# Scores in 64x64 and transposes with logits in 128x64 parts of the array, and loads requested three steps ahead

## The chip, the core and the metric

The kernel runs on one core of a Trainium2 chip. The metric is the device time of one execution in microseconds, the median of several runs. The profile is one execution taken by the hardware profiler; its times count from the start of that execution's span.

## What is computed

Three stages follow one another: decaying linear attention over 2 x 8 heads of 768 tokens, a mixture of 8 experts with one expert for each token and a capacity, and a feed-forward layer with a rational activation. The part that the change touches is the attention and the gate's logits:

```python
for t in range(S):                       # S = 768, D = 64, H = 8, B = 2
    state = gamma * state + einsum('bhd,bhe->bhde', k[:, :, t], v[:, :, t])
    y[:, :, t] = scale * einsum('bhd,bhde->bhe', q[:, :, t], state)
x = y.transpose(0, 2, 1, 3).reshape(B * S, H * D)
logits = x @ w_gate                      # then argmax, softmax, slot by count
h = relu(einsum('ecd,edf->ecf', disp, w1)); y = einsum('ecf,efd->ecd', h, w2)
h = x @ w_in; g = P(h) / Q(h); out = g @ w_out
```

## The kernel before

**Units and steps.** The attention is cut into 12 units of 128 tokens with all 8 heads (`NU` = 12, six for each batch). The loop in `attention` (L630) has one step for each unit `u`. Instructions are issued in the order in which the program writes them (`manual_schedule`), so each engine's order is the order of the calls below, and a call that waits holds back what stands behind it on its engine.

**The groups on TensorE.** For a unit there are five groups, each of matmuls in fp32 that the trace shows as two instructions each:

- `scores(u)` (L285): for four feature blocks j and two row halves r, 64 rows of k against 64 rows of q, giving 128 keys by 128 queries. Its result lies in a pair of banks ("s", for unit 1 "y"); `mask` on VectorE copies it out, and the next scores need the pair free.
- `inter(u)` (L313): the state from earlier units against q, in 64x64 parts of the array. `intra(u)` (L331): v against the masked scores, in 128x64 parts. Both add into the pair of banks "y", which `attn_xt` on VectorE reads into `xt`.
- `state(u)` (L299): k against v with 64 columns, in 128x64 parts; ACT copies it to SBUF for the next unit's inter. The last unit of a batch (u = 5) has none, and the first (u = 6) has no inter.
- `gate_mm(u)` (L351): `xt` against an identity with the gate's weights beside it (136 columns), which gives the transposed rows and the logits, in 128x128. ACT copies the logits to `lgs` and the rows to `xs` (`gate_out`), and SP stores `xs` to `xd` in HBM.

In step u the order on TensorE is scores(u+1), inter(u), intra(u), state(u), gate_mm(u-1); in steps 1 and 2 scores(u+1) come behind state(u).

**Loads.** SP's queue holds the kv loads (`attn_load`: q and k by feature in one half, v and k by token in the other, 512 KB each), the `xd` stores and the expert weights in parts of 512 KB (`load_next`, parts counted from 0, `LOADS[u]` of them in step u). A kv load of unit u+4 is written at the head of step u, into one of five buffers; it needs the buffer of unit u-1. POOL scales v of unit u+2 in step u (`scale`, L267), so a scaling that waits starts when the second half of that unit lands.

**Weights.** Each part is split in two: `split_hi` on ACT (`HI_AT`) and `split_lo` on VectorE (`LO_AT` at the head of a step, `LO_END` at its end). The six buffers of parts come free with `split_lo`.

**Routing.** The units form two groups, 0 to 6 and 7 to 11. When the logits of the first are there (step 7), VectorE works out the gate (`gate_parts`), ranks (`rank_pos`, step 8) and tables (`rank_put`, `gate_put`, step 9); `place_first` in step 10 multiplies them on TensorE (L502), copies the result out, makes the index (L533) and starts the early gather of 128 rows from `xd` on POOL (L871). Behind the loop `attn_tail` transposes these rows (`early_x`, L699), does the last gate_mm and begins with the first expert (`win_l1`, L756).

Of the kernel before, what the change touches and what calls it, by code (L numbers as in the profile page):

```python
# [7 lines left out]
F32 = mybir.dt.float32  # L8
# [16 lines left out]
NU = NT // 128  # L25
# [7 lines left out]
DEC0 = 10  # L33
LAG = (2, 3, 4, 5)
WA, WC = 7, 3
LOADS = (0, 1, 0, 1, 0, 1, 0, 2, 1, 1, 1, 2)
HI_AT = {4: (0,), 5: (1,), 8: (2,), 9: (3, 4), 10: (5,)}
LO_AT = {6: (0,), 7: (1,)}
LO_END = {9: (2,), 10: (3,), 11: (4,)}
NA = 48  # L40
LOAD_AT = {1: (34, 0), 2: (34, 1), 6: (35, 0), 7: (35, 1)}
DEC_STEPS = (14, 15, 16, 17, 18, 19, 21, 22, 25, 26, 27, 28, 29, 30, 31, 33)
# [38 lines left out]
class Build:  # L81
# [154 lines left out]
    def attn_load(self, u, c):  # L236
        nc = self.nc
        if c == 0:
            self.kv[u] = self.ap.tile([128, 4, 512], F32, tag="kv", name="kv", bufs=5)
        dst = self.kv[u][:, 2 * c : 2 * c + 2].rearrange("p w n -> p (w n)")  # L240
        nc.sync.dma_start(out=dst, in_=self.a["kv"][u, c])

# [41 lines left out]

    def scores(self, u):  # L285
        kt, qt = self.feats(u)
        sc = self.sc[u] = self.pair_bank("y" if u == 1 else "s", "sc").rearrange("p (r j t) -> p r j t", r=2, j=4)
        for j in range(4):
            for r in range(2):
                rows = slice(64 * r, 64 * r + 64)  # L290
                self.mm(sc[:, r, j], kt[rows, j], qt[rows, j], True, True)

    def mask(self, u):
        m = self.col("mask").unsqueeze(1).to_broadcast([128, 8, 128])
# [56 lines left out]
    def gate_mm(self, u):  # L351
        nc = self.nc
        xt = self.xt.pop(u)
        if u < NU - 1:
            banks = [self.bank(t, "xk") for t in ("lg", "xk")]
        else:
            y = self.pair_bank("y", "xk")
            banks = [y[:, 0:512], y[:, 512:]]
        self.xk[u] = [b[:, 0 : 2 * 136].rearrange("p (k n) -> p k n", k=2) for b in banks]
        for k in range(4):  # L360
            nc.tensor.matmul(self.xk[u][k // 2][:, k % 2], lhsT=xt[:, k], rhs=self.wi[:, k], start=True, stop=True)
        for half in range(2):
            out = self.lgs[:, u, 2 * half : 2 * half + 2]
            nc.scalar.activation(out=out, in_=self.xk[u][half][:, :, 128:], func=AF.Copy)
# [217 lines left out]
    def attention(self):  # L582
        nc, tc, a = self.nc, self.tc, self.a
        with ExitStack() as st:
            self.ap = self.pool("attn", stack=st)
            self.pa = self.pool("pa", space=PSUM, stack=st)
            self.kv, self.sc, self.scm, self.s, self.yt, self.xt = {}, {}, {}, {}, {}, {}
            self.route, self.place, self.xk, self.rk, self.where = {}, {}, {}, {}, {}
            self.qd, self.yp = {}, {}
            n0, n1 = self.cols["ident"][0], self.cols["tri"][0]  # L590
            self.ca = self.ap.tile([128, -(-n0 // 32) * 32], F32, name="ca")[:, 0:n0]
            self.wi = self.ap.tile([128, 4, 256], F32, name="wi")[:, :, 0:136]
            self.tri = self.ap.tile([128, 128], BF16, name="tri")
            self.ones = self.ap.tile([128, 128], BF16, name="ones")
            self.lgs = self.ap.tile([128, NU, 4, E], F32, name="lgs")
            self.xg0 = self.ap.tile([128, DM], F32, name="xg0")
            self.x0 = [self.ap.tile([128, 4, 128], F32R, name=n) for n in ("xh0", "xl0")]
            self.wu = self.ap.tile([128, 128], BF16, name="wu")
            nk = self.cols["gk"][0]
            self.attn_load(0, 0)  # L600
            nc.sync.dma_start(out=self.ca[:, 0:nk], in_=a["ct"][:, 0:nk])
            self.attn_part(0, 2)
            self.attn_part(0, 3)
            self.attn_load(1, 0)
            self.attn_part(1, 2)
            self.attn_part(1, 3)
            nc.sync.dma_start(out=self.ca[:, nk:n1], in_=a["ct"][:, nk:n1])
            self.attn_load(2, 0)
            nc.sync.dma_start(out=self.ct, in_=a["ct"][:, n0:])
            self.attn_load(2, 1)  # L610
            for c in range(2):
                self.attn_load(3, c)
            nc.sync.dma_start(out=self.ca[:, n1:], in_=a["ct"][:, n1:n0])
            dve, pool = nc.vector, nc.gpsimd
            dve.memset(self.wu, 0.0)
            dve.memset(self.ones, 1.0)
            self.warm(WA)
            self.scores(0)
            self.mask(0)
            for h in (0, 4):  # L620
                self.scale(0, dve, slice(h, h + 4))
            self.y_table(0, pool)
            self.scale(1, pool)
            self.y_table(1, pool)
            self.y_table(2, pool)
            self.warm(WC)
            ident = self.col("ident").unsqueeze(1).to_broadcast([128, 4, 128])
            wg = self.col("wg").rearrange("p (k e) -> p k e", e=E)
            done = {GROUPS[b + 1] - 1: b for b in range(len(GROUPS) - 1)}
            for u in range(NU):  # L630
                last = u == NU - 1
                if u + 4 < NU:
                    for c in range(2):
                        self.attn_load(u + 4, c)
                self.load_next(LOADS[u])
                if u + 2 < NU:
                    self.scale(u + 2, pool)
                if u + 3 < UPB:
                    self.y_table(u + 3, pool)
                for n in LO_AT.get(u, ()):  # L640
                    self.split_lo(n // 2, n % 2)
                if u == 0 or 2 < u < NU - 1:
                    self.scores(u + 1)
                    self.mask(u + 1)
                if u - 2 in done:
                    next(gate)
                self.inter(u)
                if u - 4 in done:
                    self.place_first()
                self.intra(u)  # L650
                if u:
                    self.attn_xt(u)
                if u - 2 in done:
                    next(gate)
                self.state(u)
                if 0 < u < 3:
                    self.scores(u + 1)
                    self.mask(u + 1)
                if u == 0:
                    self.attn_xt(0)  # L660
                    nc.scalar.activation(out=self.wi[:, :, 0:128], in_=ident, func=AF.Copy)
                    nc.scalar.activation(out=self.wi[:, :, 128:], in_=wg, func=AF.Copy)
                if u == 1:
                    nc.scalar.activation(out=self.tri, in_=self.col("tri"), func=AF.Copy)
                    nc.scalar.activation(out=self.b0a, in_=self.ab[:, 4:5], func=AF.Abs)
                    nc.scalar.activation(out=self.b1a, in_=self.ab[:, 5:6], func=AF.Abs)
                    nc.vector.memset(self.cq, 1.0 + 1e-6)
                if u:
                    self.gate_mm(u - 1)
                if u - 2 in done and not last:  # L670
                    self.rank_mm(done[u - 2])
                if u:
                    self.gate_out(u - 1, (0,))
                if u - 1 in done:
                    gate = self.gate_parts(done[u - 1])
                    next(gate)
                if u:
                    self.gate_out(u - 1, (1,))
                for n in HI_AT.get(u, ()):
                    self.split_hi(n // 2, n % 2)  # L680
                if u - 2 in done and not last:
                    self.rank_pos(done[u - 2])
                if u - 3 in done and not last:
                    self.rank_put(done[u - 3])
                    self.gate_put(done[u - 3])
                for n in LO_END.get(u, ()):
                    self.split_lo(n // 2, n % 2)
            self.attn_tail()
# [17 lines left out]

    def attn_tail(self):
        u, b = NU - 1, len(GROUPS) - 2
        self.early_x()
        self.gate_mm(u)  # L710
        self.early_lo()
# [2 lines left out]
        self.gate_group(b)  # L714
        self.gate_out(u)
        ps.append(self.pair_bank("y", "l1")[:, 0:512])
        self.load_next(1)
        self.rank_mm(b)
        self.rank_pos(b)
        self.h0 = self.wp.tile([128, 2, 512], F32, tag="wt", name="h0", bufs=3)  # L720
# [8 lines left out]
        n = E * (self.nsub + 1)  # L729
# [632 lines left out]
```

## Time and profile before

| what | us |
|---|---|
| median of 3 runs | 513.41 (513.2 to 513.69) |
| the profiled execution's time | 513.91 |
| its span | 512.1 |
| TensorE busy in the span | 500.3 (98%) |
| VectorE | 405.4 (79%) |
| ACT | 361.9 (71%) |
| POOL | 243.9 (48%) |

The span is what the profile covers; 1.8 us of the execution's time lie around it. Busy shares are means over stages of different kinds: the attention takes the first 60 us, the experts follow to about 230 us, then the feed-forward layer.

### The profile page before, as it was taken

The page shows a single profiled execution, that of the slowest core. Times are in us where ns is not written, and L with a number is a line of the kernel's source. Part 1 is how long each engine was busy: PE and PEld are TensorE (multiplying, and loading weights), DVE is VectorE, ACT ScalarE, POOL GpSimd, SP SyncE. Part 2 cuts the span into 40 slices and gives each one's busy share as a digit, 9 for nine tenths or more (in the row PEclk, how much of TensorE's full clock was granted, in tenths as well). Part 3 has the DMA queues.
Part 4 walks back from the last instruction along what each step waited for, and adds up shares of the span by engine and source line. Part 5 has one row for each costly group of instructions (what it writes and reads, how often), then busy time and mean ns, then how long its engine had stood idle before and what let it go on. Part 6 is the DMA issues. An engine that isn't in the chain of part 4 may idle for free.

```text
span 512.1 us, 9408 instructions
## 1 busy us (share of the span) xinstructions
PE 500.3 (98%) x3531; PEld 439.3 (86%) x3531; DVE 405.4 (79%) x588; ACT 361.9 (71%) x588; POOL 243.9 (48%) x187
## 2 busy tenths in 40 slices
PE   7999899999999999999999999999999999999995
PEld 4888777999999999999888888888888888888873
DVE  3468876788887978876696989999899998865973
ACT  1344537858686776855797989989899987776760
POOL 2531041033333547235354537767568765354774
PEclk9999999999999999999999999999999999999998
DMA  8999647988987999993400002222013100000203
GB/s 317 408 411 353 205 147 247 353 265 317 327 276 273 334 257 345 265 283 104 166 0 1 0 2 83 83 82 83 21 63 110 56 1 0 1 0 0 84 21 144
DMA packets 27554, 83.08 MB, mean 162 GB/s; under 512 B 4976, under 2 KB 5360, under 8 KB 27504
## 3 DMA queue, kind: packets, MB, share of 16 engines
q1 hardware_dynamic: 24448, 73.52, 42.4%
q0 software_dynamic: 2624, 7.35, 4.1%
q10 hardware_dynamic: 432, 1.57, 0.9%
q8 instruction: 28, 0.46, 0.4%
q14 instruction: 22, 0.18, 0.1%
HBM read 71.93 MB, written 10.49 MB: 161 GB/s over the span
## 4 chain that ended last, share of the span: by engine, by line
PE 65%; DVE 1%; POOL 1%; issue 1%; ACT 1%; POOLq 0%; DVEq 0%
PE h L1068 9%; PE h L1069 9%; PE h L1070 8%; PE o L1140 7%; PE o L1139 7%; PE o L1141 7%; PE l L950 3%; PE l L952 3%; PE l L979 3%; PE l L978 3%; PE l L951 3%; PE l L977 3%; POOL out L1170 1%; PE tp L921 1%; DVE fw L1105 0%
## 5 line engine op out<-in xcount | busy, mean ns | idle before, releaser
L148 DVE TENSOR_TENSOR wlo<-raw,whi 128x1024 fp32r<-128x1024 f32 x80 | 109.8, 1387 | 14.0 <-ACT whi L143 13.7
L1119 POOL TENSOR_TENSOR gg<-fx,gg 128x512 fp32r<-128x512 f32 x47 | 61.1, 1299 | 70.2 <-issue 62.4
L143 ACT ACTIVATE whi<-raw 128x1024 fp32r<-128x1024 f32 x80 | 83.2, 1054 | 3.5 <-PE l L978 3.4
L1068 PE MATMUL h<-yh,whi 128*128 128x512 f32 x192 | 74.9, 390 | 0.0
L1139 PE MATMUL o<-whi,gg 128*128 128x512 f32 x192 | 74.8, 390 | 0.0
L1070 PE MATMUL h<-yh,wlo 128*128 128x512 f32 x192 | 74.8, 389 | 0.0
L1069 PE MATMUL h<-yl,whi 128*128 128x512 f32 x192 | 74.7, 389 | 0.0
L1140 PE MATMUL o<-wlo,gg 128*128 128x512 f32 x192 | 74.7, 389 | 0.0
L1141 PE MATMUL o<-whi,gg 128*128 128x512 f32 x192 | 74.7, 389 | 0.0
L1094 POOL TENSOR_TENSOR fw<-fh,fw 128x512 f32<-128x512 f32 x48 | 64.3, 1339 | 13.5 <-ACT fw L1083 12.8
L203 POOL TENSOR_TENSOR gq<-gq 128x512 int32<-128x512 int32 x16 | 26.7, 1668 | 87.7 <-DVE gq L200 61.9
L1081 ACT ACTIVATE fx<-h,ct 128x512 f32<-128x512 f32 x48 | 37.3, 777 | 38.2 <-PE h L1070 38.1
L950 PE MATMUL l<-xh,whi 128*128 128x224 f32 x224 | 62.0, 277 | 0.1
L977 PE MATMUL l<-hh,whi 128*128 128x224 f32 x224 | 61.9, 276 | 0.0
L952 PE MATMUL l<-xh,wlo 128*128 128x224 f32 x224 | 61.5, 275 | 0.0
L979 PE MATMUL l<-hh,wlo 128*128 128x224 f32 x224 | 61.5, 274 | 0.0
L978 PE MATMUL l<-hl,whi 128*128 128x224 f32 x224 | 61.4, 274 | 0.0
L951 PE MATMUL l<-xl,whi 128*128 128x224 f32 x224 | 61.4, 274 | 0.0
L950 PEld LDWEIGHTS l<-xh,whi 128*128 128x128 f32 x224 | 43.0, 192 | 0.4 <-ACT yh L814 0.3
L978 PEld LDWEIGHTS l<-hl,whi 128*128 128x128 f32 x224 | 43.0, 192 | 0.1
L977 PEld LDWEIGHTS l<-hh,whi 128*128 128x128 f32 x224 | 43.0, 192 | 0.1
L951 PEld LDWEIGHTS l<-xl,whi 128*128 128x128 f32 x224 | 43.0, 192 | 0.0
(165 smaller groups left out, 1172.6 us busy)
## 6 DMA issues: line engine op xcount, KB each, us to landing
raw<-wm SPq DMA_DIRECT2D x61, 512.0 KB, 7.0
r<-wf SPq DMA_DIRECT2D x32, 512.0 KB, 4.9
kv<-kv SPq DMA_DIRECT2D x22, 512.0 KB, 6.9
wd<-gq SPq DMA_DIRECT2D x16, 256.0 KB, 6.2
raw<-wd SPq DMA_DIRECT2D x8, 512.0 KB, 6.5
xd<-xs SPq DMA_DIRECT2D x12, 256.0 KB, 5.4
raw<-wm ACTq DMA_DIRECT2D x3, 512.0 KB, 6.3
kv<-kv SPq DMA_DIRECT2D x4, 256.0 KB, 5.3
```

Source lines behind the costliest of these rows:

```text
L143: nc.scalar.activation(out=self.whi[i][:, sl], in_=raw, func=AF.Copy)
L148: (eng or self.nc.vector).tensor_tensor(out=self.wlo[i][:, sl], in0=raw, in1=self.whi[i][:, sl].bitcast(F32), op=ALU.subtract)
L950: nc.tensor.matmul(ps[:, fi], lhsT=wh[:, sl], rhs=xh[:, k], start=(k == 0), stop=False)
L951: nc.tensor.matmul(ps[:, fi], lhsT=wh[:, sl], rhs=xl[:, k], start=False, stop=False)
L977: mm(lhsT=wh[:, ws], rhs=fh, start=(f == 0 and o % 2 == 0), stop=False)
L978: mm(lhsT=wh[:, ws], rhs=fo, start=False, stop=False)
L1068: nc.tensor.matmul(h, lhsT=wh[:, sl], rhs=self.yh[:, k, ts], start=(k == 0), stop=False)
L1069: nc.tensor.matmul(h, lhsT=wh[:, sl], rhs=self.yl[:, k, ts], start=False, stop=False)
L1070: nc.tensor.matmul(h, lhsT=wl[:, sl], rhs=self.yh[:, k, ts], start=False, stop=(k == 3))
L1139: self.nc.tensor.matmul(ps, lhsT=gh[:, ms], rhs=wh[:, ws], start=first, stop=False)
L1140: self.nc.tensor.matmul(ps, lhsT=gh[:, ms], rhs=wl[:, ws], start=False, stop=False)
L1141: self.nc.tensor.matmul(ps, lhsT=gl[:, ms], rhs=wh[:, ws], start=False, stop=last)
```

## The change

- Scores are cut into two halves of 64 keys each, so 16 matmuls on 64x64 parts in place of 8 on 64x128; unit 1's scores go to the pair "s" as well.
- `gate_mm` is cut into two halves of 64 tokens, so 8 matmuls on 128x64 parts in place of 4 on 128x128.
- In step 0 scores(1) come behind intra(0), in step 3 scores(4) behind inter(3).
- kv loads are written three steps ahead from step 1 on, into four buffers instead of five.
- `place_first` moves from between inter and intra of step 10 to between state(10) and gate_mm(9).
- Weight loads: one moves from step 5 to 4, one from step 11 to 10, and the one of the tail to its head. `split_hi` of part 2 moves from step 8 to 6, `split_lo` of part 2 from the end of step 9 into step 7, ahead of the gate's reductions.

```diff
-LOADS = (0, 1, 0, 1, 0, 1, 0, 2, 1, 1, 1, 2)
-HI_AT = {4: (0,), 5: (1,), 8: (2,), 9: (3, 4), 10: (5,)}
+LOADS = (0, 1, 0, 1, 1, 0, 0, 2, 1, 1, 2, 1)
+HI_AT = {4: (0,), 5: (1,), 6: (2,), 9: (3, 4), 10: (5,)}
 LO_AT = {6: (0,), 7: (1,)}
-LO_END = {9: (2,), 10: (3,), 11: (4,)}
+LO_MID = {7: (2,)}
+LO_END = {10: (3,), 11: (4,)}
@@ attn_load
-            self.kv[u] = self.ap.tile([128, 4, 512], F32, tag="kv", name="kv", bufs=5)
+            self.kv[u] = self.ap.tile([128, 4, 512], F32, tag="kv", name="kv", bufs=4)
@@ scores
-        sc = self.sc[u] = self.pair_bank("y" if u == 1 else "s", "sc").rearrange("p (r j t) -> p r j t", r=2, j=4)
+        sc = self.sc[u] = self.pair_bank("s", "sc").rearrange("p (r j t) -> p r j t", r=2, j=4)
         for j in range(4):
-            for r in range(2):
-                rows = slice(64 * r, 64 * r + 64)
-                self.mm(sc[:, r, j], kt[rows, j], qt[rows, j], True, True)
+            for c in range(2):
+                keys = slice(64 * c, 64 * c + 64)
+                for r in range(2):
+                    rows = slice(64 * r, 64 * r + 64)
+                    self.mm(sc[keys, r, j], kt[rows, j, keys], qt[rows, j], True, True)
@@ gate_mm
-            nc.tensor.matmul(self.xk[u][k // 2][:, k % 2], lhsT=xt[:, k], rhs=self.wi[:, k], start=True, stop=True)
+            for c in range(2):
+                toks = slice(64 * c, 64 * c + 64)
+                self.mm(self.xk[u][k // 2][toks, k % 2], xt[:, k, toks], self.wi[:, k], True, True)
@@ attention
-                if u + 4 < NU:
+                if 0 < u < NU - 3:
                     for c in range(2):
-                        self.attn_load(u + 4, c)
+                        self.attn_load(u + 3, c)
...
-                if u == 0 or 2 < u < NU - 1:
+                if 3 < u < NU - 1:
                     self.scores(u + 1)
                     self.mask(u + 1)
...
                 self.inter(u)
-                if u - 4 in done:
-                    self.place_first()
+                if u == 3:
+                    self.scores(u + 1)
+                    self.mask(u + 1)
                 self.intra(u)
+                if u == 0:
+                    self.scores(u + 1)
+                    self.mask(u + 1)
...
+                if u - 4 in done:
+                    self.place_first()
                 if u:
                     self.gate_mm(u - 1)
...
                     self.gate_out(u - 1, (0,))
+                for n in LO_MID.get(u, ()):
+                    self.split_lo(n // 2, n % 2)
@@ attn_tail
+        self.load_next(1)
         self.early_x()
         self.gate_mm(u)
...
         ps.append(self.pair_bank("y", "l1")[:, 0:512])
-        self.load_next(1)
         self.rank_mm(b)
```

## Rows read from the trace of the kernel before

**Rows 1.** Waits of TensorE over the span: engine, line, releaser: total us, times, longest

```profile
PE sc L340 <- DMA kv<-kv: 2.2, 1, 2.2
PE tp L502 <- DVE rr L496: 1.2, 1, 1.2
PE yt L340 <- DVE xt L348: 0.7, 2, 0.5
```

**Rows 2.** Windows: stretch, us, busy of each engine, granted clock, DMA share, GB/s

```profile
40.00:45.00 5.00, 5.00 (x82) 4.49 (x82) 3.82 (x10) 1.88 (x8) 1.04 (x1) 1.00 1.02 407
...
54.00:56.00 2.00, 2.00 (x32) 1.74 (x28) 1.90 (x9) 0.57 (x2) 0.82 (x1) 1.00 0.06 23
```

**Rows 3.** Timeline of TensorE, step 7: start, us, out<-in, array part, columns, count

```profile
36.42 1.16 PE L340 MATMUL sc<-kv 64*128 64x128 f32 x16
37.51 0.67 PE L340 MATMUL yt<-kv,s 64*64 64x128 f32 x16
38.10 1.09 PE L340 MATMUL yt<-scm,kv 128*64 128x128 f32 x16
39.03 0.64 PE L340 MATMUL st<-kv 128*64 128x64 f32 x16
39.59 1.19 PE L361 MATMUL xk<-wi,xt 128*128 128x136 f32 x8
40.72 0.38 PE L340 MATMUL sc<-kv 64*128 64x128 f32 x2
```

**Rows 4.** Timeline of TensorE in narrow windows, 37.78 to 38.10

```profile
37.78 0.40 PE L340 MATMUL yt<-kv,s 64*64 64x128 f32 x8
...
37.89 0.29 PE L340 MATMUL yt<-kv,s 64*64 64x128 f32 x4
38.10 0.33 PE L340 MATMUL yt<-scm,kv 128*64 128x128 f32 x2
```

**Rows 5.** Timeline of the weight loads, step 7

```profile
38.10 0.85 PEld L340 LDWEIGHTS yt<-scm,kv 128*64 128x64 f32 x16 [0.17 <-POOL kv L267]
```

**Rows 6.** Timeline of step 0, VectorE and TensorE; brackets: idle before, releaser

```profile
6.48 0.75 DVE L267 TENSOR_TENSOR kv<-kv,ca 128x256 f32<-128x256 f32 x2
...
8.26 1.16 PE L340 MATMUL sc<-kv 64*128 64x128 f32 x16 [2.22 <-DMA kv<-kv]
```

**Rows 7.** Timeline of POOL: scaling of units 8 and 10

```profile
33.75 1.04 POOL L267 TENSOR_TENSOR kv<-kv,ca 128x512 f32<-128x512 f32 x1 [3.48 <-DMA kv<-kv]
...
42.11 1.04 POOL L267 TENSOR_TENSOR kv<-kv,ca 128x512 f32<-128x512 f32 x1 [4.17 <-DMA kv<-kv]
```

**Rows 8.** Timeline of VectorE, steps 7 to 10

```profile
41.04 0.55 DVE L393 TENSOR_REDUCE lg<-lgs 128x56 f32<-128x224 f32 x1 [1.10 <-ACT lgs L364]
...
42.24 0.98 DVE L398 TENSOR_TENSOR eq<-eq,ct 128x56 f32<-128x56 f32 x1
...
51.95 0.38 DVE L496 TENSOR_TENSOR rr<-at,gl 128x224 fp32r<-128x224 f32 x1
52.25 1.22 DVE L148 TENSOR_TENSOR wlo<-raw,whi 128x1024 fp32r<-128x1024 f32 x1
53.39 1.22 DVE L297 TENSOR_TENSOR scm<-sc,ca 128x1024 f32<-128x1024 f32 x1
...
54.73 0.15 DVE L533 TENSOR_SCALAR gidx<-tab 128x1 int32<-128x1 f32 x1
...
55.38 0.68 DVE L348 TENSOR_TENSOR xt<-yt,qd 128x512 f32<-128x512 f32 x1
```

**Rows 9.** Early gather: POOL, its landing; all gathers' landing; TensorE's transposes of it

```profile
55.17 1.20 POOL L871 DMA_INDIRECT xg<-xd,gidx  x1 [8.89 <-DVE tab L512]
...
xg<-xd,gidx POOLq DMA_INDIRECT x1, 3.6
...
DMA to landing us min/median/max: 3.4/6.5/7.6
...
58.86 0.64 PE L699 MATMUL xtp<-ct,xg 128*128 128x128 f32 x4
```

## The prediction

> **What bounds the kernel now.** I read the waits of TensorE over the whole execution first [rows 1]. They hold nearly all the time in which TensorE is not busy, about 5 us in 512.1, and all of it lies before 57 us, in the attention steps. What comes behind that point is a block that TensorE fills: its length I leave as it is, and the question is only how much earlier it starts. Its first instruction is the transposes of the early gather, at 58.86 [rows 9]. The stretches of the windows come next [rows 2]: in the attention steps the DMA engines are full (1.02 at 407 GB/s), and by 54 us they are empty (0.06). The granted clock is 1.00 in both, the 2.4 GHz level. Then step 7 of the unit loop group by group [rows 3], single groups inside it [rows 4], and last the VectorE and gather rows at the end of the attention [rows 8, 9].
>
> So three things are close to one another here: TensorE in every step, the DMA queue up to about 50 us, and VectorE from 41 to 56 us, where one instruction follows the other without idle time.
>
> **Shape changes on TensorE.** Step 7 takes 40.72 - 36.42 = 4.30 us [rows 3]. Four 64x64 pieces with 128 columns start together every 0.11 us (37.78 to 37.89 [rows 4]). At 0.11 per 128 columns the streaming alone is: scores 8 pairs x 0.11 = 0.88; inter 4 x 0.11 = 0.44; intra 8 x 0.11 = 0.88; state, 64 columns, 8 x 0.055 = 0.44; logits with transposes, 136 columns, 8 x 0.117 = 0.94; together 3.58. The other 0.72 us go to four changes of the array's shape. One can be seen: from the last inter group (37.89) to the first intra (38.10) pass 0.21 us, not 0.11 [rows 4]. Inter, entered and left by a change, takes 0.59 where it streams 0.44, so a change to 64-column weights costs 0.15; the two to 128-column weights then share 0.72 - 0.30 = 0.42, 0.21 each.
>
> After the change scores are 64x64 like inter, and the logits 128x64 like intra and state. Streaming stays: 32 score pieces in fours are 8 x 0.11, 16 logit pieces in pairs 8 x 0.117. Two changes are left (into scores, into intra), 0.30. A step falls from 4.30 to 3.88, **-0.42**. No row shows a 64x64 score. Its bounds: as inter's fours (rows 4, the same order of row halves inside column halves, the same split over banks and partitions), or, if only two ran at once, 16 x 0.11 = 1.76, +0.46 on the step. I take the fours.
>
> **The start.** Scores of unit 1 wait 2.2 us for k and q to 8.26 [rows 1, 6]; intra of unit 0 stands behind them though its v is scaled by 6.48 + 0.75 = 7.23 [rows 6]. Put ahead, its 0.93 [rows 3] fall into that wait: **-0.9**, nothing if v or the mask were late (they are not), so 0 to -0.9. Unit 1's scores move to the other pair of banks, whose reader is done by then: nothing.
>
> **Steps 1 to 6 on TensorE.** Steps 1 and 2 keep four changes, two of them narrower: -0.1 each. Step 3 saves 0.4 and the wait for the mask behind scores, 0.2. Step 4 saves 0.42, step 5 (no state) 0.4, step 6 (no inter) 0.25. With the start that is 0.9 + 0.2 + 0.6 + 1.07 = 2.8: scores of unit 8 could start at 36.42 - 2.8 = 33.6.
>
> **The loads.** Every kv load is now requested in the step after the one that requested it before, behind one more store of xd, and behind the weight load that moved up from step 5 to 4. Neither costs anything while the queue stays full, since a landing then goes by the bytes ahead; the cover is the full queue [rows 2], and if it runs dry each gap moves all that follows. At 407 GB/s 512 KB take 1.29 us, a 256 KB store 0.64. The second half of unit 8 lands at 33.75 (its scaling on POOL starts there [rows 7]), so the half with k and q at 32.46; one more weight load and one more store ahead give 34.4. So the DMA queue, not TensorE, sets step 7: **34.4, -2.0**. Unit 11: the second half of unit 10 (42.11 [rows 7]) plus one store is 42.75; two weight loads, a store and the half itself make it 42.75 + 3 x 1.29 + 0.64 = 47.3. TensorE's scores of unit 11 wait for that, which the wait for VectorE behind them (below) hides.
>
> **VectorE from step 7.** The low split of weight part 2 (parts counted from 0; 1.22, the form at 52.25 [rows 8]) moves from the end of step 9 into the 1.10 us in which VectorE waits for the logits at 41.04 [rows 8]; one change less shortens that gap by 0.2, so 0.3 stick out. The high split on ACT moves from step 8 to 6, where ACT waits for TensorE: nothing. The reductions then start at 41.04 - 2.0 - 0.1 = 38.9, **-2.1**. From there to 55.38 none of VectorE's 40 instructions has idle time ahead of it (first and last, [rows 8]); the tables are done at 51.95 + 0.38 = 52.33. So the faster TensorE of steps 8 to 10 gains nothing by itself: it waits for VectorE at the placement products, as now (1.2 [rows 1]). They stand behind state now; scores, inter, intra and state of step 10 run in the wait.
>
> **The early gather.** Before, tables, the split (1.14 to the next start), mask and copies led to the index at 54.73 + 0.15 = 54.88 [rows 8]. Now the split is gone from this chain (-1.14) but unit 10's xt stands ahead of the copies (+0.68): 54.88 - 2.1 - 1.14 + 0.68 = 52.3. The gather follows 0.29 later (55.17 [rows 9]), 52.6; it took 3.6 [rows 9] on empty DMA engines: 56.2. Here the cover is gone: weight part 8 is now requested in step 10, a step earlier, since its buffer's split no longer stands at the end of step 9. By bytes: from 42.75 eight loads (10.3) and four stores (2.6) end at 55.7, and the gather's own 0.64 gives 56.3. Both ways 56.3; the transposes start at 56.4 instead of 58.86: **-2.4**. TensorE would be there earlier: from the tables (52.33 - 2.1 = 50.2) through products (1.0), logits, inter, intra and logits (1.1 + 0.6 + 0.9 + 1.1) at 54.9. So it waits for the gather, a new wait.
>
> **The tail.** Transposes and expert weights stay 128x128, the last logits become 128x64: two changes more, 0.15 + 0.21: **+0.36**. The last weight request ahead of the final logits costs only the queue of SP, where the last xd store stands behind it; that store has until the next gathers, behind the first expert's first products. Sum -2.4 + 0.36 = **-2.0**. Within it some tenths are loose: POOL's scaling at 42.11 holds VectorE's multiply at 42.24 for 0.98 [rows 7, 8], and such meetings will fall elsewhere. Against the profiled execution: span 512.1 to 510.1, its time 513.91 to 511.9; the median of the runs is 0.5 below that one: **511.4**.
>
> **Rivals.**
> 1. *The gather meets the weight loads* (slower side). On loaded engines gathers took 6.5 in the median, 7.6 at most [rows 9]. Issued at 52.6 and landing 6.5 later, it is there at 59.1, against 58.8 now; with the tail's 0.36 that is 514.1; at 7.6, 515.2. It decides from a latency of 5.8: above, the kernel is slower. For it: weight part 8 goes out before the gather now. Against it: eight loads end by 55.7, and a gather queues only behind what is ahead of it. 18 in 100 (11 within 0.2%, 7 slower).
> 2. *The queue runs dry.* Requests a step later leave 3 us of gaps; unit 11's k and q come at 50.3, state of step 10 ends at 53.1, the index is known at about 54.6, the transposes start at 58.6, and with the tail nothing is left: 513.5. Rows 2 speak against it. 8 in 100.
> 3. *More is gained.* POOL's scaling no longer holds VectorE, and the gather is not held by loads: another 1.5, 509.9. If neither VectorE nor DMA bound anything, TensorE alone would give 2.8 + 0.4 x 3 + 1.2 = 5.2, 508.2. 10 in 100.
> 4. *The halves don't run beside each other.* If the weight loads of two column halves with the same rows were not hidden behind matmuls, the 0.85 that 16 such loads take [rows 5] would come on top of the logits in 12 steps: +10 on TensorE against its 5.2, 518. Against it: intra's 16 loads (0.85 [rows 5]) lie inside its 0.93 [rows 3]. 4 in 100, fours that run as pairs included.
>
> The Trainium skill, "TensorE: Matmul & The Clock Gate", Part 3, "The mechanism", has weight loads overlap running matmuls only where their row groups differ, which speaks against column halves of the same rows. By that rule rival 4 would be the forecast; rows 3 and 5 of this case disagree with it for intra.
>
> **How the numbers follow.** The forecast has 60 in 100, of which 8 fall within 0.2%. About 0.2%, 1 us, is what a measurement of this kernel can tell from no change. Faster: 52 + 10 = 62; within: 8 + 11 + 8 = 27; slower: 7 + 4 = 11. The range takes the gather at 6.5 us at its upper end (514.1) and rival 3 at its lower (509.9); beyond lie some 4 of rival 1 and the 4 of rival 4 above, and half of rival 3 below.
>
> **What would show it.** In the timeline of step 7 or later: scores in fours 0.11 apart, scores to inter without a gap, a step of streaming and two changes of 3.9. Scores of unit 8 waiting for a load near 34.4; the reductions near 38.9; placement products waiting for the tables; the gather issued near 52.6; TensorE waiting for it, transposes near 56.4. Wrong if that wait reaches 58.5, if scores run in pairs, if DMA shows gaps before 50 us, or if TensorE gets new waits after the transposes.

## The result and the profile after

The changed kernel takes **517.12 us** in the median of 4 runs (515.43 to 517.59), the kernel before 513.55 beside it (513.2 to 514.6): a ratio of **1.0062**, 95% interval 1.0046 to 1.0077 (the quotient of the two medians is 1.0070). It is slower, where 511.4, a gain, was forecast. The profiled execution of after is the fastest of its four: 515.43, span 513.6, against 513.91 and 512.1. So the trace explains 1.5 us of the 3.6 by which the medians differ.

What lies behind the attention steps is as long as it was: span less start of the early transposes is 513.6 - 60.20 = 453.4 after and 512.1 - 58.86 = 453.2 before [rows 9]. All is decided before 60 us, and the question is only why the transposes start 1.3 us later instead of 2.4 earlier.

Waits of TensorE over the span of after: engine, line, releaser, then total us, times, longest ("issue" is a stop for which the profile shows no releaser). They answer [rows 1].

```profile
PE sc L343 <- issue: 1.8, 3, 0.8
PE st L343 <- issue: 1.4, 1, 1.4
PE sc L343 <- DMA kv<-kv: 1.2, 2, 0.7
PE xtp L712 <- DMA xg<-xd,gidx: 1.1, 1, 1.1
...
PE rk L438 <- issue: 0.8, 1, 0.8
```

The waits of before are gone (scores of unit 1 for 2.2, placement products for 1.2). In their place stand three things that no row of before had: five stops with the releaser issue, 4.0 us together, a wait of scores for kv late in the attention (0.7, unit 11; the other of the two, 0.5, is what is left of unit 1's), and one of the transposes for the gather (1.1), which was forecast.

Timeline of TensorE in after: step 8 up to the start of step 9, which answers [rows 3]. Columns: start, us, then the instruction group.

```profile
41.07 1.10 PE L343 MATMUL sc<-kv 64*64 64x128 f32 x32
41.99 0.62 PE L343 MATMUL yt<-kv,s 64*64 64x128 f32 x16
42.54 1.09 PE L343 MATMUL yt<-scm,kv 128*64 128x128 f32 x16
43.46 0.63 PE L343 MATMUL st<-kv 128*64 128x64 f32 x16
43.93 1.10 PE L343 MATMUL xk<-wi,xt 128*64 128x136 f32 x16
44.96 0.20 PE L438 MATMUL rk<-oh,tri 128*128 128x56 bf16 x1
45.00 0.18 PE L438 MATMUL rk<-oh,ones 128*128 128x48 bf16 x1
46.01 0.28 PE L438 MATMUL rk<-oh,ones 128*128 128x40 bf16 x5 [0.82 <-issue]
```

The shapes do what was forecast. From scores to the end of the logits pass 44.96 - 41.07 = 3.89 us, where 3.88 was worked out and step 7 of before took 4.30. The 32 scores need 0.92, so they run in fours, and the 16 logit pieces 1.03. But in the middle of a group of seven small products TensorE stops for 0.82 us, waiting for no tile. The start of the kernel, which answers [rows 6], and another such stop, inside the state products of step 4:

```profile
6.88 1.09 PE L343 MATMUL yt<-scm,kv 128*64 128x128 f32 x16 [1.03 <-DVE kv L268]
8.44 0.78 PE L343 MATMUL sc<-kv 64*64 64x128 f32 x20 [0.47 <-DMA kv<-kv]
...
26.38 0.52 PE L343 MATMUL st<-kv 128*64 128x64 f32 x12
28.25 0.34 PE L343 MATMUL st<-kv 128*64 128x64 f32 x4 [1.36 <-issue]
28.38 1.15 PE L343 MATMUL xk<-wi,xt 128*64 128x136 f32 x16
```

Twelve of 16 state products run, then nothing for 1.36 us, then the last four. Counted in TensorE's records (weight loads, matmuls and its semaphore instructions), the stops that end at 21.37, 28.25, 34.38, 46.00 and 52.15 lie exactly at every 256th instruction. Of such places up to 60 us four show none: 9.59, 15.49, 39.69 and 58.57. DMA queues on the page of after, then the same row on the page of before: queue and kind, packets, MB, share.

```profile
q8 instruction: 31, 0.51, 0.4%
```

```profile
q8 instruction: 28, 0.46, 0.4%
```

Queue 8 brings TensorE's instructions, 0.51 MB in 31 packets of 16 KB. TensorE has 7732 records after and 7154 before, which is 30.2 and 27.9 times 256: so a packet holds 256 instructions of 64 B. The change needs three packets more, since the split scores and logits add 16 + 8 weight loads and as many matmuls to a step: some 198 instructions of TensorE where there were some 150.

Windows of after: stretch, us, busy of each engine, granted clock, DMA share, GB/s. The last two answer [rows 2]; below, the first stretch in the kernel before.

```profile
20.00:25.00 5.00, 4.21 (x108) 3.60 (x103) 1.82 (x2) 1.30 (x5) 1.67 (x2) 1.00 0.84 283
40.00:45.00 5.00, 5.00 (x122) 4.46 (x118) 4.86 (x12) 2.12 (x8) 1.71 (x2) 1.00 1.02 394
54.00:56.00 2.00, 2.00 (x36) 1.92 (x34) 1.14 (x4) 0.38 (x1) 0.00 (x0) 1.00 1.04 412
```

```profile
20.00:25.00 5.00, 4.80 (x79) 4.24 (x80) 2.13 (x3) 1.62 (x7) 2.20 (x3) 1.00 1.03 410
```

The granted clock is 1.00 in all, the 2.4 GHz level. But the DMA queue, full in before from 5 to 45 us (0.88 from 45 to 50), moves only 283 GB/s from 20 to 25, and is full at 54 to 56, when it used to be empty (0.06). The reason is in SyncE's queue: its DMA issues in after, then in before (start, us, instruction, count).

```profile
10.20 0.81 SPq L242 DMA_DIRECT2D kv<-kv  x2
12.03 0.33 SPq L157 DMA_DIRECT2D raw<-wm  x1
18.22 0.33 SPq L424 DMA_DIRECT2D xd<-xs  x1
18.66 0.37 SPq L242 DMA_DIRECT2D kv<-kv  x1
```

```profile
9.53 3.18 SPq L241 DMA_DIRECT2D kv<-kv  x4
13.65 0.33 SPq L156 DMA_DIRECT2D raw<-wm  x1
17.71 0.33 SPq L419 DMA_DIRECT2D xd<-xs  x1
```

In both kernels SyncE issues nothing until the first store of xd near 18 us, which waits for ScalarE. Before, four halves of kv and a weight half were asked for ahead of that pause; after, two halves and the weight half. 1 MB less lies in the queue (2.6 us at 407 GB/s), and from 21 to 23 us it moves 188 to 244 GB/s: it runs dry.

VectorE and POOL in after, which answer [rows 7, 8, 9], and the early transposes on TensorE:

```profile
38.05 1.04 POOL L268 TENSOR_TENSOR kv<-kv,ca 128x512 f32<-128x512 f32 x1 [3.20 <-DMA kv<-kv]
52.15 1.04 POOL L268 TENSOR_TENSOR kv<-kv,ca 128x512 f32<-128x512 f32 x1 [6.62 <-DMA kv<-kv]
56.16 1.20 POOL L884 DMA_INDIRECT xg<-xd,gidx  x1 [2.96 <-DVE tab L517]
```

```profile
40.40 1.22 DVE L149 TENSOR_TENSOR wlo<-raw,whi 128x1024 fp32r<-128x1024 f32 x1
41.53 0.55 DVE L398 TENSOR_REDUCE lg<-lgs 128x56 f32<-128x224 f32 x1
51.75 0.38 DVE L501 TENSOR_TENSOR rr<-at,gl 128x224 fp32r<-128x224 f32 x1
52.67 1.23 DVE L300 TENSOR_TENSOR scm<-sc,ca 128x1024 f32<-128x1024 f32 x1 [0.54 <-PE sc L343]
54.11 0.69 DVE L351 TENSOR_TENSOR xt<-yt,qd 128x512 f32<-128x512 f32 x1 [0.22 <-PE yt L343]
55.49 0.19 DVE L515 COPY tab<-tp 128x32 f32<-128x32 f32 x1 [0.69 <-PE tp L514]
55.72 0.15 DVE L538 TENSOR_SCALAR gidx<-tab 128x1 int32<-128x1 f32 x1
```

```profile
60.20 0.66 PE L712 MATMUL xtp<-ct,xg 128*128 128x128 f32 x4 [1.12 <-DMA xg<-xd,gidx]
```

The second halves of units 8 and 11 come at 38.05 and 52.15; before it was 33.75 [rows 7] and 45.24. The reductions begin at 41.53, half a microsecond later than before, not two earlier [rows 8]; and between the tables and the gather indices VectorE now has 0.54 + 0.22 + 0.69 = 1.45 us of idle time, all of it waiting for a late TensorE.

### The profile page after: what moved, and what is told of

Read it like the earlier page. It is cut to its first block, busy times and chain, and to the rows that moved or that the text cites. A ratio compares the mean times of both kernels' runs of the same rounds, so it can differ in the third digit from the quotient of the medians.

```text
span 513.6 us, 9989 instructions
## 1 busy us (share of the span) xinstructions
PE 498.3 (97%) x3819; PEld 436.7 (85%) x3819; DVE 406.0 (79%) x588; ACT 362.1 (71%) x588; POOL 245.2 (48%) x187
## 4 chain that ended last, share of the span: by engine, by line
PE 65%; DVE 1%; POOL 1%; issue 1%; ACT 1%; POOLq 0%; DVEq 0%
PE h L1081 9%; PE h L1082 8%; PE h L1083 8%; PE o L1152 7%; PE o L1153 7%; PE o L1154 7%; PE l L963 3%; PE l L965 3%; PE l L992 3%; PE l L964 3%; PE l L991 3%; PE l L990 3%; POOL out L1183 1%; PE tp L934 1%; DVE fw L1118 0%
## 6 DMA issues: line engine op xcount, KB each, us to landing
raw<-wm SPq DMA_DIRECT2D x61, 512.0 KB
r<-wf SPq DMA_DIRECT2D x32, 512.0 KB
kv<-kv SPq DMA_DIRECT2D x22, 512.0 KB
raw<-wd SPq DMA_DIRECT2D x8, 512.0 KB
raw<-wm ACTq DMA_DIRECT2D x3, 512.0 KB
```

## The experiments

Two causes were put against each other first: blocks of instructions that come too late (A), and loads requested a step later (B). Diffs are against the changed kernel unless said otherwise.

**Scores undone.** Logits stay split; a step has 166 instructions.

```
-            for c in range(2):
-                keys = slice(64 * c, 64 * c + 64)
-                for r in range(2):
-                    rows = slice(64 * r, 64 * r + 64)
-                    self.mm(sc[keys, r, j], kt[rows, j, keys], qt[rows, j], True, True)
+            for r in range(2):
+                rows = slice(64 * r, 64 * r + 64)
+                self.mm(sc[:, r, j], kt[rows, j], qt[rows, j], True, True)
```

> The changed kernel with scores in 64x128 again (one part undone; logits stay 128x64). Theory A, instruction blocks: in the changed kernel TensorE stops inside groups for 0.4 to 1.4 us with nothing to wait for, always 256 of its instructions after the last stop (705th, 961st, 1217th, 1729th, 1985th), so a block of 256 instructions comes late while the DMA engines are full. A step issues about 150 instructions before, 198 after the change, 166 here: a block then lasts 256/166 x 4.1 = 6.3 us, longer than the 5.9 to 6.9 us from one stop to the next in the changed kernel, so at most one short stop is left, and the time is 512 to 513.5. Theory B, loads requested a step later make TensorE wait: the loads are as in the changed kernel, so the time stays at 515 to 517.5.

515.88 us, ratio 1.0065 (1.0041 to 1.009). One block stop is left:

```profile
PE tp L512 <- issue: 0.5, 1, 0.5
```

Not faster all the same: scores now wait 1.8 us for kv (1.2 in after), the transposes 1.5 for the gather.

**Logits undone.** Scores stay split; a step has 182.

```
-            for c in range(2):
-                toks = slice(64 * c, 64 * c + 64)
-                self.mm(self.xk[u][k // 2][toks, k % 2], xt[:, k, toks], self.wi[:, k], True, True)
+            nc.tensor.matmul(self.xk[u][k // 2][:, k % 2], lhsT=xt[:, k], rhs=self.wi[:, k], start=True, stop=True)
```

> The changed kernel with logits and transposes in 128x128 again (scores stay 64x64). Theory A: 182 instructions in a step, a block lasts 256/182 x 4.1 = 5.8 us, so most blocks still come late, by 0.1 to 1 us each: 514 to 516, between the changed kernel and the one with scores undone. Theory B: 515 to 517.5, as the changed kernel.

517.57, ratio 1.007 (1.0046 to 1.0095), above both expectations. One stop of 0.4 us, where theory A had most blocks late; scores wait four times, 2.3 us together, for kv; the gather takes 5.4 us and TensorE waits 2.7 for it. So taking the stops away was not enough, with the late loads left in.

**Both shapes undone** (both diffs above).

> The changed kernel with both shapes undone: only the order of groups, the loads three steps ahead and the moved weight work are left. Theory A: 150 instructions in a step, a block lasts 7 us, no stop without a releaser; the start gains up to 0.9 and placement no longer waits for VectorE on the path of intra: 512 to 513.5. Theory B: the late loads are all there: 515 or more.

514.59, ratio 1.0034 (1.0017 to 1.0051), between the two expectations. No stop at all, so the stops belong to the shapes; and still slower than before. Waits of TensorE, then the window from 20 us:

```profile
PE xtp L708 <- DMA xg<-xd,gidx: 1.6, 1, 1.6
PE sc L341 <- DMA kv<-kv: 1.1, 1, 1.1
```

```profile
20.00:25.00 5.00, 5.00 (x84) 4.56 (x84) 1.93 (x3) 1.53 (x6) 2.17 (x3) 1.00 0.99 338
```

**Shapes alone**, in the kernel before: its loads, order and reductions, with the two split forms (the lines marked - in the first two diffs, in place of those marked +).

> The kernel before with both shapes and nothing else changed: loads four steps ahead, old order. Theory A: 198 instructions in a step as in the changed kernel, so stops without a releaser at every block of 256 while DMA is full, four to six of 0.4 to 1.5 us, and the 0.4 us that the shapes save in a step are eaten: 514 to 517. Theory B: nothing is requested later than before, so the shapes' gain shows: 511 to 512.5.

515.94, ratio 1.0061 (1.0042 to 1.008), with the loads of before and a full queue (408 GB/s from 20 to 25). Waits of TensorE:

```profile
PE st L342 <- issue: 1.4, 2, 0.8
PE sc L342 <- issue: 1.2, 2, 0.7
PE rk L437 <- issue: 1.2, 1, 1.2
PE yt L342 <- issue: 1.0, 1, 1.0
```

Six stops, 4.8 us, each at a 256th instruction: the shapes gain up to 0.42 a step and lose more. Cause A stands.

**Loads alone**, in the kernel before:

```
-            self.kv[u] = self.ap.tile([128, 4, 512], F32, tag="kv", name="kv", bufs=5)
+            self.kv[u] = self.ap.tile([128, 4, 512], F32, tag="kv", name="kv", bufs=4)
...
-                if u + 4 < NU:
+                if 0 < u < NU - 3:
...
-                        self.attn_load(u + 4, c)
+                        self.attn_load(u + 3, c)
```

> The kernel before with one edit of the change: k, q and v requested three steps ahead, from step 1 on, into four buffers. Shapes, order of the first step, weight loads, place_first and reductions stay as before. Theory B (the queue runs dry, and the load of a later unit comes too late): DMA share under 1.00 in 20 to 25 us (1.03 before), a wait of scores for kv of 0.7 us or more in TensorE's list, which has none before, no stops at block boundaries, and 514.3 to 515.5 us. Rival (the loads cost only where the change's other edits take away the slack): 513.1 to 513.6, as before.

515.32, ratio 1.0048 (1.0024 to 1.0073). Scores of unit 1 wait 1.5 for kv, those of unit 9 0.95, which is a new wait; two windows:

```profile
PE sc L340 <- DMA kv<-kv: 2.5, 2, 1.5
```

```profile
20.00:25.00 5.00, 4.80 (x78) 4.12 (x78) 2.26 (x3) 1.50 (x7) 2.63 (x3) 1.00 0.97 370
25.00:30.00 5.00, 5.00 (x88) 4.47 (x84) 1.92 (x2) 2.00 (x8) 1.36 (x2) 1.00 1.00 302
```

370 and 302 GB/s against 410 and 415 before are 5 x (40 + 113) = 0.77 MB less, 1.9 us at 407 GB/s. The DMA share of the second window, 1.00, hides this: by the packets' records its 4 KB packets took 225 ns in the mean, against 159 before. Cause B stands too: each edit alone makes the kernel slower, and together they cost no more than the dearer one. That fits a TensorE that waits for a load in the time that a stop has already cost, but no run here shows it by itself.

**Loads four ahead again, shapes kept** (five buffers, the last diff the other way).

> The changed kernel with k, q and v requested four steps ahead into five buffers again; both shapes stay. Theory A: the instructions are those of the change, so TensorE stops at five or six of the block boundaries for 3.5 to 6 us together, as it did when the shapes alone were put into the kernel before (six stops, 515.9 us); 515 to 516.5 us. Theory B alone (the late loads were all of it, and stops of TensorE are absorbed by the transfers): 512.5 to 513.5 us.

516.37, ratio 1.0067 (1.005 to 1.0084): nothing won. The queue is full (415 GB/s from 20 to 25), no scores wait for a load, and the stops are there (3.4 us), with a 2.4 us wait for the gather.

**Loads four ahead, both shapes undone.**

> The changed kernel with both shapes undone (scores 128x64, logits 128x128) and, beside that, k, q and v requested four steps ahead into five buffers again; what stays of the change is the order of the first step, place_first behind attn_xt, and the other places of the weight loads and of the LO reductions. Theory B (the queue runs dry at 20 to 25 us because a load three steps ahead is only requested behind a store that waits for ScalarE, and nothing makes that up): DMA share in 15 to 30 us back at 1.02 or more and 405 GB/s, the waits of scores for kv gone from the list of TensorE's waits, 512.0 to 513.0 us, so at least 1.5 us less than the kernel with three ahead (514.6). Theory D (what is left of the loss is the gather among the transfers and the weight loads, whatever the depth): the gather still lands over 4 us after its issue, TensorE waits 1 to 2 us for it, and the time stays at 514 to 515.

513.32, ratio 1.0007 (0.999 to 1.0024). The queue is full again:

```profile
20.00:25.00 5.00, 5.00 (x88) 4.51 (x82) 1.84 (x3) 1.95 (x8) 2.51 (x3) 1.00 1.03 410
```

With both causes gone the loss is gone; against the kernel above with three ahead 1.0034 falls to 1.0007 (the intervals overlap a little). The time lies above the 512 to 513 expected of B, below the 514 of its rival.

**Loads four ahead, logits split, scores not.**

> The changed kernel with scores in 128x64 again (logits stay in 128x64) and with k, q and v requested four steps ahead into five buffers. A step then issues 166 weight loads, matmuls and semaphore instructions against some 198 of the change and 150 before, so that a block of 256 lasts some 6.9 us instead of 5.9. Theory A (blocks of instructions come too late only if a block lasts less than the 5.9 to 6.9 us from a boundary to the next block's arrival): at most one stop of TensorE with the releaser issue. Theory B: no wait of scores for kv, DMA share 1.02 or more in 15 to 30 us. By both together 511.5 to 513.0 us, the best of the variants. If 514 or more, the loss sits in neither, and the gather among the weight loads (lands 4.4 us after its issue in the kernel with three ahead) carries it.

512.59, ratio 0.9996 (0.998 to 1.0012). 166 instructions a step, and no stop over 0.1 us where a block begins; the transposes start at 56.99, 1.9 earlier than before. The median shows only a part of this.

**What delays a block.** The kernel with the shapes alone, with five weight halves not loaded, so that its time is not compared:

```
-        (eng or self.nc.sync).dma_start(out=raw, in_=src[:, sl])
+        if i * 2 + half < 5:
+            self.nc.gpsimd.memset(raw, 0.01)
+        else:
+            (eng or self.nc.sync).dma_start(out=raw, in_=src[:, sl])
```

> The kernel before with both shapes and with the first five half loads of expert weights left out, a constant filled in by GpSimd in their place, so that 2.5 of the first expert's 6 weight parts are not the reference's and their transfers are not on the queue. The instructions of TensorE in the attention phase are the same as with the shapes alone. Theory A with its reason (a block's transfer is late because it stands among full DMA queues): from the boundary to the block's arrival well under the 5.9 to 6.9 us, and the six stops (1.22, 0.86, 0.97, 1.03, 1.36, 0.78 us) shrink to one or none in the stretch where the queue is no longer full. Rival (the stop belongs to the instructions themselves, or to a fixed latency of the fetch): the stops stay at about 1 us each. The total time is not to be compared, as loads are left out.

Of the six places four show 0.2 us or less, two 1.60 and 1.58. At these two the block's packet began 4.75 and 4.60 us after the boundary (the 256th place before), at the others 1.4 to 2.6. That is neither one theory's number nor the other's, so a stronger form was made: the kernel with the shapes alone, with k, q and v of seven units not loaded (v is formed from k there).

```
+        if u > 4:
+            self.kv[u] = self.kv[u - 5]
+            return
...
+        w = self.toks(u)[1][:, h] if u > 4 else v
...
```

> The kernel before with both shapes, with the transfers of k, q and v left out for units 5 to 11, which use the tiles of units 0 to 4 again (v is formed from k times its factor there, so the values of these units are not the reference's); the number of TensorE instructions is unchanged. From 27 us on only the stores of xd and the weight halves are on the DMA queues. Theory A with its reason (a block of 256 instructions is fetched late because its transfer stands behind full queues): the stops up to 27 us stay, and of the boundaries at some 28, 34, 40, 46 and 53 us, where the kernel with the shapes alone stops for 0.86, 0.97, 1.03, 1.36 and 0.78 us, none stops for over 0.2 us; the fetch starts under 2.5 us after the boundary (3.0 to 4.3 us there). Rival (a fetch takes so long whatever the queues hold): stops of about 1 us stay at each. The total time is not to be compared, as loads are left out.

No stop over 0.2 us anywhere, not even before 27 us, where stops were expected to stay; the queue is below 370 GB/s from 15 us on. The weight loads and matmuls of TensorE are as many as with the shapes alone (3819 each); "issue" is no longer among its waits. A window of it, with 99 GB/s where the kernel with the shapes alone moved 413:

```profile
25.00:30.00 5.00, 5.00 (x126) 4.47 (x120) 2.98 (x3) 2.24 (x6) 1.31 (x2) 1.00 0.27 99
```

Put side by side, from the records of queue 8 and of TensorE: when an instruction at a 256th place ran, how much later the next packet on queue 8 began, when that packet ended, and when the next 256th instruction was reached and ran. Reached is the start of the record before it, so a stop is a little longer here than the idle time that the profile gives.

```
kernel            ran    packet began  ended   next reached  ran    stop
before            35.14  +3.69         39.77   43.00         43.01  none
changed           21.37  +4.69         27.02   26.67         28.25  1.58
changed           28.25  +3.93         33.15   33.49         34.38  0.89
changed           34.38  +2.57         37.90   39.64         39.69  none
shapes alone      41.24  +4.35         46.46   46.56         47.93  1.37
5 halves left out 28.30  +4.75         34.01   33.62         35.22  1.60
5 halves left out 42.16  +2.09         45.14   47.46         47.48  none
k, q, v left out  31.90  +0.93         34.47   37.21         37.22  none
```

The instruction behind a stop runs 1.2 to 1.7 us after the packet's end, in all the kernels. In the changed kernel the packet takes 0.9 to 1.0 us and starts 2.5 to 4.7 us after the boundary; 0.2 to 1.8 from 21 us on where k, q and v are left out. So from a boundary to the next block 5 to 7 us pass in the changed kernel. A block of 256 lasted 7.0 to 8.1 us before, and lasts 4.8 to 5.5 with both shapes, stops left out: before it was always in time. So much is shown: with k, q and v left out a packet starts early. But a full queue is not all that makes it late, since the latest start in the changed kernel (4.69) lies in 21 to 26 us, where the queue moves 188 to 412 GB/s; what else does is open.

**The low split of weight part 2 moved** (the third LO reduction of the expectation), out of step 7 to behind the gather indices, in the kernel with loads four ahead and logits split:

```
-LO_MID = {7: (2,)}
-LO_END = {10: (3,), 11: (4,)}
+LO_MID = {}
+LO_END = {10: (3, 2), 11: (4,)}
```

> The kernel with logits in 128x64, scores in 128x64 and loads four ahead (512.6), with one reduction moved: the third LO reduction stands in step 10 behind the tables and the gather indices, no longer in step 7 behind gate_mm. In the trace of that kernel VectorE has no idle time from 37.9 us, where this reduction (1.22 us) stands, to the gather indices at 52.5 us, and TensorE then waits 1.7 us for the gather. Theory C (VectorE's chain sets the gather, and the gather sets the end): the indices 1.2 us earlier, at 51.3, the gather landing at 55.7, TensorE out of other work at 55.3, so its wait shrinks to some 0.5 us and the time by 1.2 us, to 511.4. Rival (the gather has to pass more transfers the earlier it is issued, or the reduction is missed later by win_l1): no gain, 512.6.

511.76, ratio **0.9959** (0.9945 to 0.9973): faster than both kernels. VectorE near the reductions, without and with the move:

```profile
37.88 1.22 DVE L149 TENSOR_TENSOR wlo<-raw,whi 128x1024 fp32r<-128x1024 f32 x1
39.01 0.54 DVE L396 TENSOR_REDUCE lg<-lgs 128x56 f32<-128x224 f32 x1
```

```profile
39.48 0.55 DVE L396 TENSOR_REDUCE lg<-lgs 128x56 f32<-128x224 f32 x1 [0.92 <-ACT lgs L367]
```

The trace bears the reason out in part only. Without the 1.22 us VectorE waits 0.92 for the logits, so TensorE bounds it there; the indices stand at 52.75, not 51.3, in an execution whose first scores took 2.08 us instead of 1.16. The transposes wait 1.2 for the gather instead of 1.7. That execution is the slowest of the kernel's six.

**The same without the split logits.**

> The fastest variant so far (0.9959 of the kernel before: loads four ahead, third LO reduction behind the gather indices, logits in 128x64, scores in 128x64) with the logits back in 128x128, so that no new shape is left. If the logits' shape is worth what the streaming and the changes of the array's shape say (two changes less in a step, some 0.2 us, of which VectorE's chain from 39 us on hides the later ones), scores of unit 8 start some 0.6 us later and the time is 0.5 to 1.0 us over that variant, at 0.997 to 0.998 of the kernel before. If VectorE's chain hides all of it, the ratio is the same, 0.996. If the shape costs something by its additional instructions (166 in a step against 150), this kernel is faster.

511.82, ratio **0.9964** (0.9953 to 0.9976): the same. So no part of the gain that these runs can tell comes from a new shape. That VectorE's chain hides what the logits' shape saves, as expected for this outcome, its trace does not show: VectorE still waits 1.1 us for the logits ahead of the reductions. Against the same kernel with the split in step 7 (1.0007) the move alone is worth 0.4%.

## Why the prediction was wrong

Two steps of the prediction failed: the shapes were given no price for their additional instructions, and the later loads were put at nothing on the ground of a full queue. The rest follows from these two, or held.

**What bounds the kernel** was read rightly: every trace keeps 453 us behind the early transposes (453.0 to 453.8 where all loads are made, but 454.7 with the logits undone, at a mean granted clock of 0.994), and the gather does set their start. All errors are ahead of it. One figure was misread: TensorE is not busy for 512.1 - 500.3 = 11.8 us, not 5; 5.3 of it lie before 60 us, and 6.2 at 505 us and later, behind its last products (6.3 in after).

**Shapes, -0.42 a step: the size held, a term was missing.** Step 8 measured 3.89 for 3.88, with the scores in fours (32 in 0.92 us). The working counted streaming and shape changes and took the number of instructions as free. 48 more per step are the term that was left out: 4.0 us of stops in after, about as much as all steps together could gain at the 0.1 to 0.42 each of the prediction. Rows of before showed the ingredients (queue 8 in the page, a full DMA queue), but no stop, since its blocks lasted 7 us and more. The Trainium skill, "Runtime: NRT & Kernel Launch", section "Instruction fetch mechanics", describes it: instructions come in 16 KiB blocks of 256, the next one fetched by DMA while the current one runs. The traces agree with block and count. It calls the crossing "mostly hidden"; here it is hidden in the kernel before and costs 0.4 to 1.4 us a block in the changed one.

**The start, -0.9: right in size.** Intra of unit 0 runs at 6.88 inside the wait. Scores of unit 1 then wait 0.47 for their load, and scores of unit 2 start at 12.72 for 13.48, -0.76.

**The loads, "neither costs anything while the queue stays full": the step that failed beside the shapes.** The condition was named, and it did not hold. I supported it with a window at 40 to 45 us [rows 2], and did not look at SyncE's pause from 14 to 17.7 us, where a request one step later falls behind a store that waits for ScalarE. That is rival 2, which got 8 in 100 and 3 us of gaps. The runs show such gaps, of 1.9 us in two windows of the loads alone, and 512.4 to 513.6 of span (512.1 before) in all kernels with three ahead but one (516.0, the logits undone). Scores of unit 8 started at 37.18, not 34.4: the three stops up to there are 2.8 us, and with the stops gone but the late loads kept (both shapes undone) they start at 36.7, behind a wait of 1.1 for the load; with the loads four ahead but the stops kept, at 36.4, as before. Either cause alone takes the forecast's 2.0.

**VectorE.** The reductions at 41.53 instead of 38.9 follow from that. From there to the last table it took 51.75 - 41.53 = 10.2 us (10.9 before). The low split put into the gap of step 7 fills it, as forecast: no idle time stands ahead of it or behind it in after. Its cost shows once TensorE is fast: 0.4% between the kernels with and without it there, where the forecast counted 0.3 us.

**Placement products and indices.** Forecast: TensorE waits for the tables at 50.2. In fact the tables, done at 51.75 + 0.38 = 52.1, wait for TensorE: scores of unit 11 wait 0.70 for their load, stop 0.39 for a block, and the products come at 54.45, so the indices are done at 55.87 instead of 52.3. The gather, 4.0 us for 3.7, was the term that held: **rival 1**, which needed 5.8, did not occur in after (5.4 came nearest, with the logits undone). The queue was full up to just before the gather (1.04 at 54 to 56, 0.59 at 56 to 57); it took 0.4 us more than before.

**The tail, +0.36**, was 453.4 - 453.2 = 0.2. **Rival 4** fell: 16 logit pieces in column halves of the same rows take 1.03 us, so they run in pairs beside each other, as intra does. The rule of the Trainium skill cited with it does not hold here as it was put; its section excepts loads into the background weight buffer, and no run here tells where these go.

**What stays open.** The median of after lies 1.7 us above its own trace, and kernels with late loads or block stops scatter more (514.1 to 519.3 with the loads alone) than the two fastest (510.8 to 512.1); but the one with both undone does so too (512.0 to 515.9), and so does the kernel before (512.4 to 515.7 beside the loads alone). Why is not settled, since only one execution of each has a trace. Nor is it settled why moving one split is worth 0.4% when its trace shows a smaller shift.

## What to carry to other kernels

Splitting a matmul over parts of the array keeps the streaming and doubles the instructions: count them between two arrivals of a 256-instruction block and compare that time with what a fetch takes among the DMA traffic of the same stretch, here 5 to 7 us from a boundary to the next block. Before shortening a prefetch by a step, find the longest pause in the issuing queue (here SyncE behind a store) and count the bytes that lie ahead of it; a window that is full later proves nothing. And where two edits each cost, undoing one of them can show nothing: here both had to go before the time came back.

## What the hardware showed that was not expected

TensorE stops for 0.4 to 1.4 us at a multiple of 256 instructions (weight loads counted) when the next block's packet, which starts 2.5 to 4.7 us after the last boundary in the changed kernel, ends less than 1.2 us before the block is reached, or later; the profile calls this wait "issue". With 99 to 268 GB/s on the queues (20 to 50 us, k, q and v left out) the same instructions show none over 0.2 us. In some executions (the one shown of the moved reduction among them) the first 16 scores took 2.08 us instead of 1.16 at a granted clock shown as 1.00; this costs 0.9 us there, and no run here tells why.
